# A fused attention and GeGLU kernel: a split opening of the first gate phase, a spare accumulator, and new orders of the attention steps

## The chip, the cores and the metric

The kernel runs on one core of a Trainium2 chip. The metric is the device time of one execution in microseconds (us). Two times are given for it: the median of three plain runs, and the time of one execution that was recorded with a profile. Every row of the profile belongs to that one execution.

## What is computed

Causal attention with 16 always visible "beacon" keys in front, for 8 batches of 8 heads, 576 tokens and head width 64; its output, as 4608 tokens of width 512, goes through a gated feed-forward block with inner width 1536.

```
k_all, v_all = concat([beacon_k, k]), concat([beacon_v, v])
scores = q @ k_all.T / sqrt(64); causal part masked to -1e9
a = softmax(scores)                      # rows sum to 1
x = (a @ v_all) -> tokens x 512
g, val = x @ w_gate, x @ w_val           # 512 -> 1536
out = (gelu(g) * val) @ w_out            # 1536 -> 512
```

## The kernel before, in words

**Tiling.** Tokens are cut into 9 chunks of 512 for the feed-forward part, while attention runs over 8 batches of 576 tokens, so after batch b chunk b is complete. Heads go in four pairs per batch (m = 0 to 3); the two heads of a pair occupy two halves of the array. A chunk's gate phase makes 12 tiles, each of 4 matmuls with `wg_sb` and 4 with `wv_sb` into a two-bank accumulator `gv_ps`; ScalarE takes the Gelu of one bank (`ge_sb`), VectorE multiplies the other by it into `hT_sb` (`gate_val_mms`, `gate_val_end`, lines 365 to 390). The output projection is counted in units of one matmul `o_ps`: 12 units make one output tile of 128 tokens, which VectorE copies to `o_sb` (line 426) and SyncE stores; a chunk has 48 units.

**Attention of a pair** is a list of steps written in strings, one string ("slot") for each pair and one last slot. The letters (function `attention`, line 451):

- `S0` to `S3`: one of four chunks of transposed scores into `s_ps`, then its exp on ScalarE into `expT`. Widths per head are 512, 480, 464 and 208. `s0`, `s2`, `s3` put the scores into the accumulator with the tag `z` instead of the pool `psum_s`.
- For batches from 2 on, GpSimd masks the diagonal blocks behind each exp (line 294). In batches 0 and 1 the masks are steps of their own: `a13` is pair 1, chunk 3 on GpSimd, `d00` one on VectorE by a table.
- `Z`: row sums of the pair before (matmuls with `ones` into `z_ps`, 12, and two with `v_sb`); `I`: their inverse on VectorE (two transposes and a reciprocal); `V`: values into `x_ps`; `M`: the scaling of both into `xT_sb` (line 355). A digit gives the pair.
- `O12`: 12 output units of earlier chunks. `N3`: the next three loads of q and k for the next batch, issued by GpSimd. `h1o`: one matmul `heat` whose result nobody reads.
- `k1z`, `q1x`, `k2o`: TensorE transposes of k or q of one pair for batch 1, into the bank named last; VectorE copies them to `qkT`. From batch 2 on, transposing DMAs on SyncE's queue do this (`xbar_transpose`), issued after the opening of the gate phase.

**Accumulators.** The eight PSUM banks are: pool `psum_s`, two buffers of two banks in turn, for scores and gate tiles; `psum_x`, one buffer `z` of two banks (sums) and one `x` of one bank (values); `psum_o`, one bank `o`. A buffer is free again when its last reader is done.

**Order.** Every engine runs its instructions in the order in which the code issues them. `gate_val_first` (line 397) opens a gate phase: it issues the matmuls of the first `tiles` tiles that need pairs 0 to 2 only, then a filling (`heat` or `o`) of n, then the matmuls that need pair 3. `gate_val` issues whole tiles. GpSimd's queue carries masks and all loads; a load is issued by the instruction at line 115, which waits until the semaphore that it takes from a round of eight is free.

The lines concerned: 365 to 370 (choice of the accumulator of a gate tile), 545 to 552 (gate phase of chunk 0 with two transposes of batch 1, `load_v(1)` and `load_out_w()`), 554 to 571 (the strings of batches 1, 2 and 3 to 7 and the opening of their gate phases), 572 (what is left of the output units).

Of the kernel before, what the change touches and what calls it, by code (L numbers as in the profile page):

```python
# [7 lines left out]
P = 128  # L8
# [5 lines left out]
F_TILES = D_FF // P  # L14
K_CHUNKS = D_MODEL // P
CH = 512
# [29 lines left out]
Z0 = 448  # L46
# [3 lines left out]
FP32 = mybir.dt.float32  # L50
# [8 lines left out]
def kernel(  # L59
# [22 lines left out]
    psum_s = ctx.enter_context(tc.tile_pool(name="psum_s", bufs=2, space=bass.MemoryType.PSUM))  # L82
    psum_x = ctx.enter_context(tc.tile_pool(name="psum_x", bufs=1, space=bass.MemoryType.PSUM))
# [30 lines left out]
    def dma(out_ap, in_ap):  # L114
        keep(nc.gpsimd.dma_start(out=out_ap, in_=in_ap))  # L115
# [8 lines left out]
    def load_runs(b, m):  # L124
        for out_ap, in_ap in runs(b, m):
            dma(out_ap, in_ap)
# [70 lines left out]
    def load_out_w():  # L197
        dma(wo_sb, moe_w_out.rearrange("(ii p) m -> p ii m", p=P))
# [3 lines left out]
    def mm(out_ap, lhsT, rhs, start, stop, **kw):  # L202
        keep(nc.tensor.matmul(out_ap, lhsT, rhs, start=start, stop=stop, **kw))  # L203
# [48 lines left out]
    def trans_in(tag, b, m, w):  # L252
        t_ps = bank(tag, BF16, 1024, "t_ps")
        trans(b, m, w, t_ps, [(S, dve_copy)])
# [3 lines left out]
    def scores(b, m, *chunks, tag="s"):  # L258
        i = b * NPAIR + m
        qkT = qk_ring[b % 2]  # L260
        for c in chunks:
            if c == 0:
                exp_of[i] = epool.tile([P, 2, EXP_W], BF16, name="expT", tag="expT")
            expT = exp_of[i]
            s_ps = (psum_s if tag == "s" else psum_x).tile([P, 2, 512], FP32, name="s_ps", tag=tag)
            for t, s_lo, w, col in CHUNKS[c]:
                for hi in range(2):
                    r = slice(64 * hi, 64 * hi + 64)
                    mm(
                        s_ps[:, hi, col : col + w],  # L270
                        qkT[r, 1, m, t * P : (t + 1) * P],
                        qkT[r, 0, m, NB + s_lo : NB + s_lo + w],
                        True,
                        True,
                    )
            o, w = CHUNK_OFF[c], CHUNK_W[c]
            act(expT[:, :, o : o + w], s_ps[:, :, 0:w], ACT.Exp, scale=QK_SCALE)
            if b > 1:
                mask(b, m, c)
# [42 lines left out]
    def sums(b, m):  # L322
        z_ps = z_of[b * NPAIR + m] = psum_x.tile([P, 1024], FP32, name="z_ps", tag="z")
        attend(b, m, z_ps, Z0, True, 0, SPLIT)
        attend(b, m, z_ps, Z0 + SPLIT, True, SPLIT, S)
        attend(b, m, z_ps, 0, False, 0, SPLIT, start=False)

    def values(b, m):
        x_ps = x_of[b * NPAIR + m] = psum_x.tile([P, S - SPLIT], FP32, name="x_ps", tag="x")
        attend(b, m, x_ps, 0, False, SPLIT, S)  # L330
# [3 lines left out]
    def invert(b, m):  # L334

        i = b * NPAIR + m
        zt = npool.tile([P, S], FP32, name="zt", tag="zt")
        keep(nc.vector.transpose(zt, z_of[i][:, Z0 : Z0 + S]))  # L338
        rz = npool.tile([P, NBLK], FP32, name="rz", tag="rz")
        keep(nc.vector.reciprocal(rz, zt.rearrange("p (n j) -> p n j", j=32)[:, :, 0]))  # L340
        rec = npool.tile([P, S], FP32, name="rec", tag="rec")
        keep(
            nc.vector.transpose(  # L343
                rec.rearrange("p (n j) -> p n j", j=32), rz.unsqueeze(2).to_broadcast([P, NBLK, 32])
            )
        )
        rec_of[i] = rec
# [15 lines left out]
    h_of, gv_of = {}, {}  # L363

    def gate_val_mms(ci, fi, kks):
        if fi == 0 and ci not in h_of:
            h_of[ci] = hpool.tile([P, F_TILES, CH], BF16, name="hT_sb", tag="hT_sb")
        if (ci, fi) not in gv_of:
            gv_of[ci, fi] = psum_s.tile([P, 2, CH], FP32, name="gv_ps", tag="s")
        gv_ps = gv_of[ci, fi]  # L370
        for w in range(2):
            for kk in kks:
                mm(
                    gv_ps[:, w, :],
                    (wg_sb, wv_sb)[w][:, kk, fi * P : (fi + 1) * P],
                    xT_sb[:, kk, ci * CH : (ci + 1) * CH],
                    kk == 0,
                    kk == K_CHUNKS - 1,
                    skip_group_check=True,
                )  # L380

    def gate_val_end(ci, fi):
        gv_ps = gv_of.pop((ci, fi))
        ge_sb = fpool.tile([P, CH], BF16, name="ge_sb", tag="ge_sb")
        act(ge_sb, gv_ps[:, 0, :], ACT.Gelu)
        keep(
            nc.vector.tensor_tensor(  # L387
                out=h_of[ci][:, fi, :], in0=gv_ps[:, 1, :], in1=ge_sb, op=ALU.mult
            )
        )  # L390

    def gate_val(ci, f0, f1):
        for fi in range(f0, f1):
            gate_val_mms(ci, fi, range(K_CHUNKS))
            gate_val_end(ci, fi)

    def gate_val_first(ci, fill, n, tiles=1):

        for fi in range(tiles):
            gate_val_mms(ci, fi, range(K_CHUNKS - 1))  # L400
        fill(n)
        for fi in range(tiles):
            gate_val_mms(ci, fi, [K_CHUNKS - 1])
            gate_val_end(ci, fi)
# [46 lines left out]
    def attention(b, *slots, extra=None):  # L451


        for m, slot in enumerate(slots):
            for step in slot.split():
                kind, n = step[0], step[1:]
                if kind == "S":
                    scores(b, m, *(int(c) for c in n))
                elif kind == "s":
                    scores(b, m, *(int(c) for c in n), tag="z")  # L460
                elif kind == "Z":
                    sums(b, int(n or m - 1))
                    if not n:
                        invert(b, m - 1)
                elif kind == "I":
                    invert(b, int(n))
                elif kind == "V":
                    values(b, int(n or m - 1))
                    if not n:
                        scale(b, m - 1)  # L470
                elif kind == "M":
                    scale(b, int(n))
                elif kind == "O":
                    o(int(n))
                elif kind in "adkq":
                    extra[kind](b, *n)
                else:
                    extra[kind](*n) if kind in "kqrwLhyad" else extra[kind](n)
# [40 lines left out]
    def load_next(n):  # L519
# [4 lines left out]
    extra = {  # L524
        "k": lambda b, m, tag: trans_in(tag, b, int(m), 1),
        "q": lambda b, m, tag: trans_in(tag, b, int(m), 0),
        "a": lambda b, m, c: mask(b, int(m), int(c)),
        "d": lambda b, m, c: mask(b, int(m), int(c), by_table=True),
        "r": lambda m: load_runs(0, int(m)),
        "h": lambda n, tag: heat(int(n), tag),  # L530
        "y": lambda t: load_v_tile(0, int(t)),
        "N": lambda n: load_next(int(n)),
# [3 lines left out]
    for m in range(1, NPAIR):  # L536
# [4 lines left out]
        extra=extra,  # L541
    )
    load_next(99)
    gelu_table()
    gate_val_first(0, heat, 0, 1)
    gate_val(0, 1, 10)
    trans_in("z", 1, 0, 1)
    gate_val(0, 10, 10 + 1)
    trans_in("x", 1, 0, 0)
    gate_val(0, 10 + 1, F_TILES)  # L550
    load_v(1)
    load_out_w()

    for b in range(1, B):
        exp_table()
        if b + 1 < B:
            queue.extend(qk_loads(b + 1))
        if b == 1:
            attention(b, "S0 N3 k1z S1 a01 q1x k3o d00 S2 a02 S3 q2o d03", "N3 S0 S1 k2o Z0 a11 S2 a10 I0 a12 V0 S3 M0", "S0 a13 q3o S1 a21 Z1 S2 h1o a20 I1 S3 a22 V1", "M1 S0 S1 a23 Z2 I2 a31 a30 V2 M2 S2 a32 S3 a33 O12", "Z3 I3 V3 M3 O12 N3", extra=extra)
        elif b == 2:  # L560
            attention(b, "S0 O12 N3 S1 S2 O12 S3 N3", "S0 Z0 S1 S2 I0 O12 S3 N3 V0", "S0 S1 M0 Z1 V1 S2 S3 O6 I1", "S0 M1 S1 Z2 V2 I2 S2 M2 S3", "O2 O4 Z3 V3 I3 N2 M3 O12", extra=extra)
        else:
            attention(b, "O1 s0 S1 O11 s2 S3 N3", "S0 O2 Z0 I0 S1 V0 S2 S3 M0 O10", "S0 S1 Z1 I1 N3 V1 M1 S2 S3 O12", "S0 S1 Z2 V2 S2 I2 S3 M2 N2 O7", "Z3 I3 V3 N3 M3", extra=extra)
        gelu_table()
        if b + 1 < B:
            load_next(99)
            load_v(b + 1)
        gate_val_first(b, o, 0 if b == 1 else 0 if b == 2 else 5)
        if b + 1 < B:
            xbar_transpose(b + 1)  # L570
        gate_val(b, 1, F_TILES)
# [36 lines left out]
```

## Time and profile before

| | us |
|---|---|
| median of three runs | 401.12 |
| lowest and highest of them | 400.2 and 401.52 |
| profiled execution | 399.99 |
| its span, from first to last instruction | 398.3 |

The span is cut below by the start of each phase on TensorE, read from its timeline:

| phase | from | to |
|---|---|---|
| start and attention of batch 0 | 0 | 24.23 |
| gate phase of chunk 0, with two transposes | 24.23 | 47.05 |
| attention of batch 1 | 47.05 | 69.62 |
| gate phase of chunk 1 | 69.62 | 90.44 |
| attention of batch 2 | 90.44 | 115.17 |
| attention of batch 4 | 178.58 | 199.62 |
| after the gate phase of batch 7 | 350.34 | 398.3 |

In the profile PE is TensorE's matmuls, PEld its weight loads, ACT ScalarE, DVE VectorE, POOL GpSimd, SP SyncE. A row of a timeline gives the start, the time to the end of the last of the merged instructions, the engine, the line, the operation, out<-in, the shape of the first, the number of instructions, and in brackets the idle time before it with what ended it. Matmuls are pipelined, so their durations overlap: the distance between starts is what each costs in a run.

These are the costliest groups of ScalarE and VectorE in the attention and gate phases (busy us, mean ns of one, idle before and its releaser):

```profile
L387 DVE TENSOR_TENSOR hT_sb<-gv_ps,ge_sb 128x512 bf16<-128x512 f32 x108 | 74.7, 692 | 116.2 <-ACT ge_sb L206 116.2
L206 ACT ACTIVATE expT<-s_ps 128x1024 bf16<-128x1024 f32 (+3 forms) x128 | 102.8, 865 | 31.9 <-PE s_ps L203 29.0
L338 DVE STREAM_TRANSPOSE zt<-z_ps 128x576 f32<-128x576 f32 x32 | 25.1, 783 | 28.4 <-PE z_ps L203 28.2
```

### The profile page before, as it was taken

The page shows a single profiled execution, that of the slowest core. Times are in us where ns is not written, and L with a number is a line of the kernel's source. Part 1 is how long each engine was busy: PE and PEld are TensorE (multiplying, and loading weights), DVE is VectorE, ACT ScalarE, POOL GpSimd, SP SyncE. Part 2 cuts the span into 40 slices and gives each one's busy share as a digit, 9 for nine tenths or more (in the row PEclk, how much of TensorE's full clock was granted, in tenths as well). Part 3 has the DMA queues.
Part 4 walks back from the last instruction along what each step waited for, and adds up shares of the span by engine and source line. Part 5 has one row for each costly group of instructions (what it writes and reads, how often), then busy time and mean ns, then how long its engine had stood idle before and what let it go on. Part 6 is the DMA issues. An engine that isn't in the chain of part 4 may idle for free.

```text
span 398.3 us, 6685 instructions
## 1 busy us (share of the span) xinstructions
PE 382.4 (96%) x2633; PEld 178.3 (45%) x2674; DVE 197.9 (50%) x339; ACT 188.5 (47%) x255; POOL 164.4 (41%) x299
## 2 busy tenths in 40 slices
PE   7889989999999999999999999999999999999996
PEld 3444444444444444444444444444444444444443
DVE  4863677433663356434653356336643465433332
ACT  4843485236733574338723763357434862322210
POOL 8967268305870078405770379107840330000000
PEclk9999989999999999999999999999999999999999
DMA  9999995945999059994799179915997010000012
GB/s 145 158 206 178 156 96 56 148 86 81 107 113 131 7 81 86 133 112 55 93 128 135 30 72 130 159 21 81 93 161 77 28 53 28 0 26 28 26 59 102
DMA packets 139424, 36.50 MB, mean 92 GB/s; under 512 B 126976, under 2 KB 134912, under 8 KB 139392
## 3 DMA queue, kind: packets, MB, share of 16 engines
q0 software_dynamic: 103696, 18.85, 61.4%
q1 hardware_dynamic: 35552, 17.08, 20.8%
q8 instruction: 21, 0.34, 0.4%
q10 hardware_dynamic: 144, 0.13, 0.1%
q14 instruction: 11, 0.09, 0.1%
HBM read 38.27 MB, written 9.44 MB: 120 GB/s over the span
## 4 chain that ended last, share of the span: by engine, by line
PE 86%; ACT 7%; DVE 3%; issue 1%; DMA 1%; POOL 1%; POOLq 0%
PE gv_ps L203 47%; PE o_ps L203 20%; PE z_ps L203 8%; PE s_ps L203 6%; PE x_ps L203 5%; ACT expT L206 5%; ACT L446 2%; DMA k<-in_k_dram 1%; DVE zt L338 1%; DVE rec L343 1%; ACT ge_sb L206 1%; PE t_ps L224 1%; DVE xT_sb L355 0%; POOL q L115 0%; DVE rz L340 0%
## 5 line engine op out<-in xcount | busy, mean ns | idle before, releaser
L206 ACT ACTIVATE ge_sb<-gv_ps 128x512 bf16<-128x512 f32 x108 | 64.5, 597 | 155.7 <-PE gv_ps L203 153.4
L387 DVE TENSOR_TENSOR hT_sb<-gv_ps,ge_sb 128x512 bf16<-128x512 f32 x108 | 74.7, 692 | 116.2 <-ACT ge_sb L206 116.2
L294 POOL TENSOR_SCALAR_AFFINE_SELECT expT<-expT 128x256 bf16<-128x256 bf16 (+2 forms) x156 | 57.3, 394 | 154.4 <-ACT expT L206 152.5
L206 ACT ACTIVATE expT<-s_ps 128x1024 bf16<-128x1024 f32 (+3 forms) x128 | 102.8, 865 | 31.9 <-PE s_ps L203 29.0
L203 PE MATMUL gv_ps<-xT_sb,wg_sb 128*128 128x512 bf16 x422 | 111.1, 379 | 1.2 <-DVE xT_sb L355 0.8
L203 PE MATMUL gv_ps<-xT_sb,wv_sb 128*128 128x512 bf16 x425 | 111.0, 379 | 0.5
L203 PE MATMUL o_ps<-wo_sb,hT_sb 128*128 128x512 bf16 (+1 forms) x421 | 100.2, 374 | 1.4 <-issue 0.3
L203 PEld LDWEIGHTS <-wv_sb 128*128 128x128 bf16 x432 | 42.3, 98 | 51.9 <-issue 1.0
L203 PEld LDWEIGHTS <-wg_sb 128*128 128x128 bf16 x432 | 41.6, 98 | 50.8 <-issue 1.6
L203 PEld LDWEIGHTS <-hT_sb 128*128 128x128 bf16 x444 | 40.8, 98 | 47.7 <-issue 3.7
L426 DVE COPY o_sb<-o_ps 128x512 f32<-128x512 f32 x35 | 24.2, 690 | 39.6 <-PE o_ps L203 39.6
L203 PE MATMUL s_ps<-qkT 64*128 64x80 bf16 (+5 forms) x384 | 38.7, 283 | 4.7 <-ACT expT L206 3.5
L338 DVE STREAM_TRANSPOSE zt<-z_ps 128x576 f32<-128x576 f32 x32 | 25.1, 783 | 28.4 <-PE z_ps L203 28.2
L115 POOL DMA_DIRECT2D v_sb<-in_v_dram x40 | 33.8, 886 | 0.0
L203 PE MATMUL z_ps<-expT,ones 80*64 80x80 bf16 (+5 forms) x384 | 31.8, 292 | 1.4 <-DVE xT_sb L355 0.2
L203 PEld LDWEIGHTS <-qkT 64*128 64x128 bf16 x384 | 14.4, 94 | 32.0 <-issue 26.8
L203 PE MATMUL x_ps<-expT,v_sb 128*64 128x512 bf16 (+4 forms) x320 | 28.1, 305 | 0.0
L115 POOL DMA_DIRECT2D q_sb<-in_q_dram x30 | 26.0, 865 | 0.5 <-issue 0.2
L115 POOL DMA_DIRECT2D k_sb<-in_k_dram x30 | 25.8, 860 | 0.2 <-issue 0.2
L343 DVE STREAM_TRANSPOSE rec<-rz 128x576 f32<-128x576 f32 x32 | 24.9, 778 | 1.1
L203 PEld LDWEIGHTS <-ones 128*64 128x64 bf16 (+1 forms) x384 | 15.7, 112 | 16.9 <-issue 8.6
L355 DVE TENSOR_TENSOR xT_sb<-x_ps,rec 128x512 bf16<-128x512 f32 x32 | 21.8, 681 | 0.8 <-PE x_ps L203 0.8
(39 smaller groups left out, 122.2 us busy)
## 6 DMA issues: line engine op xcount, KB each, us to landing
out_dram<-o_sb SPq DMA_DIRECT2D x35, 256.0 KB, 2.0
v_sb<-in_v_dram POOLq DMA_DIRECT2D x24, 128.0 KB, 7.2
q_sb<-in_q_dram POOLq DMA_DIRECT2D x24, 128.0 KB, 4.3
k_sb<-in_k_dram POOLq DMA_DIRECT2D x18, 128.0 KB, 4.3
wg_sb<-in_moe_w_gate_dram POOLq DMA_DIRECT2D x3, 512.0 KB, 8.9
wv_sb<-in_moe_w_val_dram POOLq DMA_DIRECT2D x3, 512.0 KB, 10.6
wo_sb<-in_moe_w_out_dram POOLq DMA_DIRECT2D x1, 1536.0 KB, 14.3
q<-in_q_dram POOLq DMA_DIRECT2D x7, 144.0 KB, 5.3
```

Of the source, the lines that this page charges most:

```text
L115: keep(nc.gpsimd.dma_start(out=out_ap, in_=in_ap))
L203: keep(nc.tensor.matmul(out_ap, lhsT, rhs, start=start, stop=stop, **kw))
L206: keep(nc.scalar.activation(out_ap, in_ap, func, **kw))
L224: keep(nc.tensor.transpose(out_ap, in_ap, ident[0:n, 0:n]))
L294: nc.gpsimd.affine_select(out=d, in_=d, pattern=[[0, 2], [1, DIAG[t]]], compare_op=ALU.is_ge, fill=0.0, base=base, channel_multiplier=-1,)
L338: keep(nc.vector.transpose(zt, z_of[i][:, Z0 : Z0 + S]))
L343: nc.vector.transpose(rec.rearrange("p (n j) -> p n j", j=32), rz.unsqueeze(2).to_broadcast([P, NBLK, 32]))
L355: nc.vector.tensor_tensor(out=xT_sb[:, m, b * S + q0 : b * S + q1], in0=acc[:, 0 : q1 - q0], in1=rec[:, q0:q1], op=ALU.mult,)
L387: nc.vector.tensor_tensor(out=h_of[ci][:, fi, :], in0=gv_ps[:, 1, :], in1=ge_sb, op=ALU.mult)
L426: keep(nc.vector.tensor_copy(o_sb, o_ps))
L446: keep(nc.scalar.preload_act_table_set(SET_EXP))
```

## The change

A third tile of chunk 0's gate phase, (0, 2), takes its accumulator from the buffer `z` of `psum_x`. The gate phase of chunk 0 opens with two split tiles for one; the transposes of batch 1's first pair stand two tiles earlier; `wo_sb` is loaded before the values of batch 1. The strings of batches 1, 2 and 3 to 7 are new, one `heat` matmul of batch 1 is dropped, and the gate phase of batch 2 opens with a filling of 5 output units for 0.

```diff
--- before
+++ after
@@ -366,7 +366,10 @@
         if fi == 0 and ci not in h_of:
             h_of[ci] = hpool.tile([P, F_TILES, CH], BF16, name="hT_sb", tag="hT_sb")
         if (ci, fi) not in gv_of:
-            gv_of[ci, fi] = psum_s.tile([P, 2, CH], FP32, name="gv_ps", tag="s")
+            spare = (ci, fi) == (0, 2)
+            gv_of[ci, fi] = (psum_x if spare else psum_s).tile(
+                [P, 2, CH], FP32, name="gv_ps", tag="z" if spare else "s"
+            )
         gv_ps = gv_of[ci, fi]
         for w in range(2):
             for kk in kks:
@@ -542,30 +545,30 @@
     )
     load_next(99)
     gelu_table()
-    gate_val_first(0, heat, 0, 1)
-    gate_val(0, 1, 10)
+    gate_val_first(0, heat, 0, 2)
+    gate_val(0, 2, 8)
     trans_in("z", 1, 0, 1)
-    gate_val(0, 10, 10 + 1)
+    gate_val(0, 8, 8 + 1)
     trans_in("x", 1, 0, 0)
-    gate_val(0, 10 + 1, F_TILES)
+    gate_val(0, 8 + 1, F_TILES)
+    load_out_w()
     load_v(1)
-    load_out_w()
 
     for b in range(1, B):
         exp_table()
         if b + 1 < B:
             queue.extend(qk_loads(b + 1))
         if b == 1:
-            attention(b, "S0 N3 k1z S1 a01 q1x k3o d00 S2 a02 S3 q2o d03", "N3 S0 S1 k2o Z0 a11 S2 a10 I0 a12 V0 S3 M0", "S0 a13 q3o S1 a21 Z1 S2 h1o a20 I1 S3 a22 V1", "M1 S0 S1 a23 Z2 I2 a31 a30 V2 M2 S2 a32 S3 a33 O12", "Z3 I3 V3 M3 O12 N3", extra=extra)
+            attention(b, "k1x S0 N3 S1 a01 k3z d00 q1x S2 a02 s3 q2o d03", "S0 S1 k2o Z0 a11 S2 I0 a12 V0 a10 M0 S3", "a13 S0 q3o S1 a21 Z1 S2 a20 I1 S3 a22 V1", "M1 S0 S1 a23 Z2 I2 V2 a31 M2 a30 S2 a32 S3 d33 O12", "Z3 I3 V3 M3 O12 N3 N3", extra=extra)
         elif b == 2:
-            attention(b, "S0 O12 N3 S1 S2 O12 S3 N3", "S0 Z0 S1 S2 I0 O12 S3 N3 V0", "S0 S1 M0 Z1 V1 S2 S3 O6 I1", "S0 M1 S1 Z2 V2 I2 S2 M2 S3", "O2 O4 Z3 V3 I3 N2 M3 O12", extra=extra)
+            attention(b, "O12 s0 S1 S2 O12 S3 N3", "S0 S1 Z0 I0 V0 M0 S2 S3 O12 N3", "S0 S1 Z1 I1 V1 M1 S2 S3 O12 N3", "S0 S1 Z2 I2 V2 M2 S2 S3 O12 N2", "Z3 I3 V3 M3", extra=extra)
         else:
-            attention(b, "O1 s0 S1 O11 s2 S3 N3", "S0 O2 Z0 I0 S1 V0 S2 S3 M0 O10", "S0 S1 Z1 I1 N3 V1 M1 S2 S3 O12", "S0 S1 Z2 V2 S2 I2 S3 M2 N2 O7", "Z3 I3 V3 N3 M3", extra=extra)
+            attention(b, "O7 s0 S1 S2 O12 S3 N3", "S0 S1 Z0 I0 V0 M0 S2 S3 O12 N3", "S0 S1 Z1 I1 V1 M1 S2 S3 O7 N3", "S0 S1 Z2 I2 V2 M2 S2 S3 O5 N2", "Z3 I3 V3 M3", extra=extra)
         gelu_table()
         if b + 1 < B:
             load_next(99)
             load_v(b + 1)
-        gate_val_first(b, o, 0 if b == 1 else 0 if b == 2 else 5)
+        gate_val_first(b, o, 0 if b == 1 else 5 if b == 2 else 5)
         if b + 1 < B:
             xbar_transpose(b + 1)
         gate_val(b, 1, F_TILES)
```

## The prediction

> **What bounds the kernel now.** I read the page, then the chain of waits, then busy time by stage, then the timeline of each engine around every edited string.
>
> ```profile
> PE 382.4 (96%) x2633; PEld 178.3 (45%) x2674; DVE 197.9 (50%) x339; ACT 188.5 (47%) x255; POOL 164.4 (41%) x299
> PE 86%; ACT 7%; DVE 3%; issue 1%; DMA 1%; POOL 1%; POOLq 0%
> ```
>
> TensorE is the bound: 96% busy and 86% of the chain that ended last. Nothing in the edit removes matmuls worth naming (one `heat` matmul in all), so any gain is gaps in TensorE's stream. The stages show where they are; the columns are window, its length, then busy us (count) of PE, PEld, DVE, ACT, POOL, then clock and DMA. The rows are the attention of batches 1, 2, 4 and 5:
>
> ```profile
> 47.05:69.62 22.57, 20.74 (x244) 10.96 (x245) 16.86 (x33) 15.90 (x19) 14.08 (x28) 0.92 0.91 87
> 90.44:115.17 24.73, 24.02 (x202) 11.17 (x206) 13.96 (x25) 16.22 (x19) 18.75 (x35) 1.00 0.88 92
> 178.58:199.62 21.04, 20.50 (x185) 9.40 (x187) 11.29 (x20) 16.01 (x19) 13.48 (x28) 1.00 0.60 70
> 221.43:242.67 21.24, 20.70 (x186) 9.41 (x187) 11.31 (x20) 16.01 (x19) 13.49 (x28) 1.00 0.59 69
> ```
>
> "Busy" includes pipeline tails, so it hides small gaps. The timeline of TensorE in batch 4 shows them (start, us, what, idle before):
>
> ```profile
> 178.58 0.38 PE L203 MATMUL o_ps<-wo_sb,hT_sb 128*128 128x512 bf16 x1
> 178.89 0.60 PE L203 MATMUL s_ps<-qkT 64*128 64x512 bf16 x8
> 179.42 2.55 PE L203 MATMUL o_ps<-wo_sb,hT_sb 128*128 128x512 bf16 x11
> 181.90 0.46 PE L203 MATMUL s_ps<-qkT 64*128 64x464 bf16 x4
> 182.62 0.39 PE L203 MATMUL s_ps<-qkT 64*128 64x512 bf16 x2 [0.26 <-ACT expT L206]
> 182.95 0.39 PE L203 MATMUL o_ps<-wo_sb,hT_sb 128*128 128x512 bf16 x1
> 183.48 1.14 PE L203 MATMUL z_ps<-expT,ones 128*64 128x64 bf16 x12
> ...
> 189.04 0.91 PE L203 MATMUL z_ps<-expT,ones 128*64 128x64 bf16 x12
> 189.81 0.85 PE L203 MATMUL x_ps<-expT,v_sb 128*64 128x512 bf16 x10
> 190.59 0.61 PE L203 MATMUL s_ps<-qkT 64*128 64x464 bf16 x4
> ```
>
> In a run, full matmuls start every 0.216 us (179.42 to 181.90: eleven, 2.38, plus 0.10). From one output matmul at 178.58 to the scores at 178.89 is 0.31: so **a switch to or from scores costs 0.10 us**. The same 0.10 stands wherever kinds change, except from row sums to values. Clean blocks of a pair: first two score chunks 0.43, sums 0.77, values 0.68, last two chunks 0.28: 2.16, so 8.64 for four pairs; 43 output matmuls 9.28; sum 17.92 of 21.04. The missing 3.1 are 18 switches (1.8) and waits (1.3): 0.43 before 182.62, 0.22 (beyond its switch) before 183.48, 0.2 inside those sums (they last 0.97 to the next row, not 0.77), the rest small.
>
> The opening of chunk 0's gate phase, and the clock in batch 1:
>
> ```profile
> 24.89 0.81 PE L203 MATMUL gv_ps<-xT_sb,wv_sb 128*128 128x512 bf16 x3
> 26.45 0.38 PE L203 MATMUL gv_ps<-xT_sb,wg_sb 128*128 128x512 bf16 x1 [0.76 <-DVE xT_sb L355]
> ```
>
> ```profile
> 52.79:56.20 3.41, 3.41 (x36) 1.87 (x36) 2.19 (x5) 2.35 (x3) 3.09 (x6) 0.50 1.42 93
> ```
>
> Six matmuls (1.29) cannot cover the scaling of pair 3; and 3.41 us of batch 1 run at half clock.
>
> **The skill.** "TensorE: Matmul & The Clock Gate", Part 1, says that an idle activity window of about 3.4 us halves the clock, and that windows are not tied to the kernel's start; the 3.41 us at 0.50 agrees. Part 2 there says that weight loads are pulled ahead of running matmuls when row groups don't conflict or the background buffer takes them; here the 98-ns loads vanish in a run and a like amount (0.10) shows at switches. "DMA: Bandwidth & Descriptors", section "Queues, rings and completion order", says descriptors of a ring are consumed in ring order; the trace agrees: k_sb's first rows, issued 1.0 us after wo_sb, landed just behind it (after 13.5 us, wo_sb after 14.3).
>
> **The change, part by part.**
>
> *Gate opening, chunk 0.* Twelve matmuls now precede the first that needs pair 3: 24.23+2.59=26.82, and DVE delivers at 25.72+0.68=26.40. The gap before 26.45 (0.92: start 25.53 due after six) goes. Next late could be tile 3, which needs tile 0's psum_s slot: tile 0 ends 27.25, Gelu 27.45 to 28.05, multiply to 28.77; tile 2 sits in the z bank (read last by the scaling at 25.6 to 25.8), so tile 3 starts only at 29.41. No wait. Gain **0.92**. Moving the two transposes two tiles earlier is free: their loads landed by 34.3, they start at 38.0.
>
> *wo_sb before v.* The same POOL issues (1.06 for wo_sb, 4.7 for v), so issue time is nil. But POOL reuses eight DMA semaphores in turn: in the built order k_sb's first tile now waits for wo_sb's. Such a wait is visible before:
>
> ```profile
> 30.29 0.63 POOL L115 DMA_DIRECT2D k<-in_k_dram  x1 [1.92 <-DMA wg_sb<-in_moe_w_gate_dram]
> 39.08 1.06 POOL L115 DMA_DIRECT2D wo_sb<-in_moe_w_out_dram  x1
> ```
>
> Issued at 34.4 with 14.3 to land, wo_sb lands near 48.8; then two issues (0.88+0.94) free POOL at 50.6. Queued behind: masks a01 and a02, whose exps end at 50.0 and 50.9, needed by Z0 at 51.8. They fit, by some 0.1. v follows wo_sb in the rings: its loads landed between 38.8 and 43.2 before, 4.4 apart, so the last near 53.3, and values of pair 0 want it at 53.4. Nothing, or up to 1 us late; below nothing is excluded, since v was never late. I take 0.
>
> *Batch 1.* Gate ends at 46.03 (46.95 less 0.92). k1x moves ahead of S0: 46.13 to 46.62, in time that was idle before S1 (0.60 idle at 48.53, waiting for the last Gelu's multiply; that wait stays, to 47.60). Exp starts at 48.14 (Gelu, table 1.28), and exps follow each other by 0.92, 0.85, 0.82, 0.40 (1.89 for the first two together, 1.35 for the last two, less 0.1 overlap): c3 ends 51.27. s3 in the z bank no longer waits for exp c1. S0 of pair 1 waits for q1's copy (DVE: multiply, k1, k3, d00, q1: 50.43): 50.48. k2o to 51.73, Z0 51.83, V0 53.05, S0 of pair 2 54.12, Z1 55.10, V1 56.65, S0 of pair 3 57.45, Z2 58.30, V2 59.13, O12 60.3 to 62.9, Z3 to 64.5, O12 to 67.2. Gate of chunk 1 at 67.2 for 69.62; less the 0.92: **1.5**, at full clock. The eight q/k loads now issued last end at 68.3 (before 68.6), so the transposes, done at about 14 us of SP issue after 71, stay well before batch 2. If a window of 46.8 to 50.2 (by this walk about 0.4 streaming, like the 0.38 that fell before) trips the clock, 1.2 of it comes back.
>
> *Batches 3 to 7.* New order: O7, s0 S1 S2, O12, S3 S0 S1, Z0 V0 and so on: 16 switches for 18 (-0.2). New waits, from the gate's end: O7 to 1.51; its copy on DVE 1.72 to 2.41, so O12 starts at 2.46 for 2.34 (0.12). O12 to 5.05, S3 5.15; its exp 5.42 to 5.96, because S3 stands behind O12; S1 of pair 1 needs that slot: 6.00 for 5.45 (0.55). Z0 then finds all masks. Small ones as before (0.3 to 0.4). Gone are 0.43+0.22+0.21. Sum: 1.6+0.12+0.55+0.4=2.7 for 3.1 to 3.2: about **0.5** each, 2.6 for five. Cover that shrinks: O5 for O7 before Z3 (0.43 less); Z3 at 18.85 needs scaling of pair 2 (18.6) and the last mask. POOL there is dense: from 6.0, a mask, then N3 (2.6) and five masks (1.75) per slot give 19.5 for the last mask, needed at 19.49. Costs 0 to 0.4 each; I take 0. Fill and pair 3's scaling keep their distance (Z3 moves both).
>
> *Batch 2.* Same walk with O12 first: exp starts 1 us later, hidden by output matmuls; waits 0.15 and 0.55; switches 16. Its gaps were 3.2, now 2.7: **0.5**. Five outputs more here (89 done for 84) are five fewer after batch 7 (7 for 12): nil.
>
> Sum 0.9+1.5+0.5+2.6=**5.5**. The profiled execution took 399.99 (span 398.3), so 394.5; the timed runs' median is 401.12, 1.13 above it, so 395.6, which I predict.
>
> **Rivals.**
> *Half clock or late v in batch 1 again.* For: the new slot 0 still idles about 1.5 us in pieces while exps run. Against: fewer, shorter pieces. 1.2 to 2 back: 397.2.
> *The new waits eat the reordering.* Z3 (or Z1, Z2) wait 0.4 each for masks behind N3: batches 2 to 7 give almost nothing; 2.4 to 3 saved: 398.4. For: 0.1 margins. Against: DMA issues were steady at 0.88.
> *Slower: POOL becomes the late engine.* Masks of a slot stand behind N3. If each issue takes longer or waits for its semaphore, the sums of slots 1 to 4 wait. It decides when it costs more than the 5.5 saved plus 1.2: 6.7 over five batches with loads (2 to 6), 1.35 each, 0.45 per late slot. For: 4.4 us of POOL per slot beside 4.1 of TensorE in the short slots. Against: 13.48 of 21.04 busy. Price 2 us each: 405.6.
> *The spare bank gives nothing* (tile 2 waits anyway): 0.9 lost, 396.5; the z bank's reads end a microsecond earlier, so unlikely.
>
> **Numbers.** Forecast 0.52 (own range 393.6 to 396.8), clock or v 0.23, eaten 0.14, slower 0.07, spare bank 0.04. Range 392.8 to 399.2: the lower end is waits of 0.3 per batch that don't appear and a faster batch 1, the upper holds the two mild rivals. A measurement tells 0.3% (1.2 us) from no change. Faster 0.87, same 0.06, slower 0.07.
>
> **What would show it.** Right: the gate's wait near 26.45 gone and its start unmoved; batch 1's attention near 21.2 with clock 1.00; periods of batches 3 to 6 (42.86 from 135.92 to 178.78) near 42.3; a 0.5 us wait before the second scores of slot 1, none before the first. Wrong: sums waiting for POOL, scores of batch 1 behind v or masks after wo_sb, or a half-clock window at other places.

## The result and the profile after

| us | before | after |
|---|---|---|
| median of six runs each, on one chip | 401.15 | 396.45 |
| lowest and highest | 400.2 and 401.52 | 395.41 and 399.06 |
| ratio, with 95% interval | 1 | 0.9898 [0.9866, 0.9931] |
| profiled execution (span) | 399.99 (398.3) | 399.06 (397.3) |

A run over 1.5% above the fastest of the same kernel counts as slow and is left out of the ratios and medians here, which concerns three runs of experiment 3 alone.

The profiled execution of the changed kernel was the longest of its six, so the two profiles differ by 0.93 us only where the medians differ by 4.7. Reading the two spans alone would mislead; the phases show why. The table cuts both executions at the first gate matmul of each chunk, read from TensorE's timeline.

| stretch on TensorE, us | before | after | saved |
|---|---|---|---|
| start to gate phase of chunk 0 | 24.23 | 28.34 | -4.11 |
| gate phase of chunk 0 | 22.72 | 21.80 | 0.92 |
| its end to gate phase of chunk 1 (batch 1) | 22.67 | 20.91 | 1.76 |
| gate 1 to gate 2 | 45.38 | 44.96 | 0.42 |
| gate 2 to gate 3 (after: five output units, 1.08, more) | 41.77 | 42.54 | 0.31 like for like |
| gate 3 to gate 4 | 42.85 | 42.53 | 0.32 |
| gate 4 to gate 5 | 43.05 | 42.54 | 0.51 |
| gate 5 to gate 6 | 42.85 | 42.53 | 0.32 |
| gate 6 to gate 7 | 42.85 | 42.38 | 0.47 |
| gate 7 to the end (after: the five units fewer) | 69.90 | 68.81 | 0.01 like for like |

All edited stretches together saved 5.0 us. The stretch ahead of them, whose code is identical in both kernels, took 4.11 us more in this one execution. These rows of TensorE's timeline show the reason, first of the kernel before and then of the one after:

```profile
15.59 0.88 PE L203 MATMUL x_ps<-expT,v_sb 128*64 128x512 bf16 x10
...
20.23 0.85 PE L203 MATMUL x_ps<-expT,v_sb 128*64 128x512 bf16 x10
```

```profile
13.19 1.60 PE L203 MATMUL z_ps<-expT,ones 128*64 128x64 bf16 x12
...
18.60 1.55 PE L203 MATMUL x_ps<-expT,v_sb 128*64 128x512 bf16 x10
...
21.15 0.85 PE L203 MATMUL x_ps<-expT,v_sb 128*64 128x512 bf16 x10
```

The same ten value matmuls take 0.85 to 0.88 us, and 1.55 in the second kernel up to about 20.9 us: TensorE ran at half its clock there. Note that the clock column does not say so. The busy table of the changed kernel by stage follows (window, length, busy us and count of PE, PEld, DVE, ACT, POOL, then clock and DMA); its rows are the start, the gate phase of chunk 0, and the attention of batch 1:

```profile
5.00:20.90 15.90, 15.27 (x164) 8.16 (x161) 9.04 (x18) 10.20 (x14) 13.11 (x24) 1.00 1.31 133
28.34:50.14 21.80, 21.80 (x123) 9.84 (x121) 10.97 (x19) 6.46 (x11) 12.09 (x18) 1.00 1.39 190
50.14:71.05 20.91, 19.10 (x244) 10.05 (x244) 16.90 (x34) 15.81 (x19) 11.87 (x25) 1.00 0.64 52
```

The first row reads 1.00 although its matmuls last nearly double: the column counts as full what lies before the first clock record. The gate phase is now busy for all of its 21.80 us, and batch 1's attention runs at full clock throughout, where before 3.41 us of it were at 0.50.

The two lines of the page that answer to those of before, busy time and the chain that ended last:

```profile
PE 386.0 (97%) x2673; PEld 179.7 (45%) x2673; DVE 197.7 (50%) x340; ACT 188.4 (47%) x255; POOL 163.1 (41%) x298
...
PE 91%; DVE 4%; ACT 2%; DMA 1%; issue 1%; SPq 0%
```

PE's part of the chain went from 86% to 91% and ACT's from 7% to 2%: exps and the Gelu stand less often in the chain that ended last. They still stop TensorE: its waits that an exp ended sum to 3.7 us in 11 places, for 3.5 us in 12 places before, since batches 3 to 7 each lost one such wait and got another. (PE's 386.0 is more than the 382.4 of before in part because matmuls at half clock count as busy for longer: 15.27 us from 5.00 to 20.90, for 13.32 in the kernel before.)

The opening of chunk 0's gate phase, on TensorE's timeline:

```profile
29.64 0.81 PE L203 MATMUL gv_ps<-xT_sb,wg_sb 128*128 128x512 bf16 x3
30.29 0.81 PE L203 MATMUL gv_ps<-xT_sb,wv_sb 128*128 128x512 bf16 x3
30.94 0.38 PE L203 MATMUL gv_ps<-xT_sb,wg_sb 128*128 128x512 bf16 x1
```

The second tile's six matmuls fill the place of the gap, and the first matmul that needs pair 3 starts at 30.94, right behind (0.65 after 30.29), with no wait in brackets.

Attention of batch 4, the same engine; before it began with one output unit, now with seven:

```profile
180.36 1.68 PE L203 MATMUL o_ps<-wo_sb,hT_sb 128*128 128x512 bf16 x7
181.97 0.79 PE L203 MATMUL s_ps<-qkT 64*128 64x512 bf16 x10
182.81 2.75 PE L203 MATMUL o_ps<-wo_sb,hT_sb 128*128 128x512 bf16 x12
185.50 0.48 PE L203 MATMUL s_ps<-qkT 64*128 64x208 bf16 x4
186.37 0.38 PE L203 MATMUL s_ps<-qkT 64*128 64x64 bf16 x6 [0.39 <-ACT expT L206]
...
188.24 0.46 PE L203 MATMUL s_ps<-qkT 64*128 64x464 bf16 x4
...
193.40 0.61 PE L203 MATMUL s_ps<-qkT 64*128 64x464 bf16 x4
...
198.19 1.25 PE L203 MATMUL o_ps<-wo_sb,hT_sb 128*128 128x512 bf16 x5
199.37 1.06 PE L203 MATMUL z_ps<-expT,ones 128*64 128x64 bf16 x12
200.24 0.19 PE L203 MATMUL z_ps<-expT,v_sb 128*64 128x64 bf16 x1
```

The wait before the third scores is gone. One new wait stands in brackets, before the second scores of pair 1 (186.37), as large as walked. Three small ones have to be computed: 181.97 to 182.81 is 0.84, about 0.1 more than the scores and a switch need; the pair of last chunks takes 0.15 longer in the rows of 0.61 than in that of 0.46; the last sums take 0.87 (199.37 to 200.24) where clean ones take 0.74.

### The profile page after: what moved, and what is told of

It is laid out like the page before. It is cut to its first block, busy times and chain, and to the rows that moved or that the text cites. A ratio compares the mean times of both kernels' runs of the same rounds, so it can differ in the third digit from the quotient of the medians.

```text
span 397.3 us, 6726 instructions
## 1 busy us (share of the span) xinstructions
PE 386.0 (97%) x2673; PEld 179.7 (45%) x2673; DVE 197.7 (50%) x340; ACT 188.4 (47%) x255; POOL 163.1 (41%) x298
## 4 chain that ended last, share of the span: by engine, by line
PE 91%; DVE 4%; ACT 2%; DMA 1%; issue 1%; SPq 0%
PE gv_ps L203 47%; PE o_ps L203 24%; PE z_ps L203 7%; PE s_ps L203 6%; PE x_ps L203 5%; ACT expT L206 2%; PE t_ps L224 1%; DVE o_sb L429 1%; DMA p<-in_k_dram 1%; DVE rec L343 1%; DVE zt L338 1%; DVE xT_sb L355 0%; DVE qkT L247 0%; PE heat L203 0%; DVE rz L340 0%
## 5 line engine op out<-in xcount | busy, mean ns | idle before, releaser
L294 POOL TENSOR_SCALAR_AFFINE_SELECT expT<-expT 128x256 bf16<-128x256 bf16 (+2 forms) x155 | 56.4, 395 | 152.3 <-ACT expT L206 150.3
L203 PE MATMUL gv_ps<-xT_sb,wg_sb 128*128 128x512 bf16 x432 | 112.4, 379 | 0.0
L203 PE MATMUL gv_ps<-xT_sb,wv_sb 128*128 128x512 bf16 x432 | 112.4, 379 | 0.0
L203 PE MATMUL o_ps<-wo_sb,hT_sb 128*128 128x512 bf16 (+1 forms) x444 | 101.8, 374 | 0.3
L203 PEld LDWEIGHTS <-hT_sb 128*128 128x128 bf16 x444 | 41.8, 98 | 48.8 <-issue 3.5
L203 PE MATMUL z_ps<-expT,ones 80*64 80x80 bf16 (+5 forms) x384 | 30.8, 294 | 0.7 <-DVE xT_sb L355 0.6
```

The source lines that it names most:

```text
L294: nc.gpsimd.affine_select(out=d, in_=d, pattern=[[0, 2], [1, DIAG[t]]], compare_op=ALU.is_ge, fill=0.0, base=base, channel_multiplier=-1,)
```

## The experiments

Each kernel is the changed kernel with the edit shown, unless a base is named; experiments 9 to 11 each keep the edits of the one before. The medians, with the ratio to the kernel before, run beside them:

| edit | median us (runs) | ratio [95%] |
|---|---|---|
| 1 opening undone | 397.71 (4) | 0.9887 [0.9799, 0.9974] |
| 2 no spare bank | 396.42 (4) | 0.9893 [0.9811, 0.9974] |
| 3 old strings in batch 1 | 397.86 (17 of 20) | 0.9917 [0.9889, 0.9945] |
| 4 old strings in batches 2 to 7 | 398.81 (20) | 0.9944 [0.992, 0.9969] |
| 5 v before wo_sb | 397.15 (6) | 0.9912 [0.9878, 0.9947] |
| 6 fourth chunk earlier | 394.75 (4) | 0.9842 [0.9816, 0.9869] |
| 7 one warming matmul at the start for seven | 397.46 (7) | 0.9915 [0.9882, 0.9948] |
| 8 edits 6 and 5 | 396.97 (6) | 0.9886 [0.9851, 0.9921] |
| 9 edit 8, first output units in another bank | 394.58 (6) | 0.9844 [0.9816, 0.9872] |
| 10 edit 9, unread matmuls in batch 1 | 394.71 (6) | 0.9839 [0.9808, 0.987] |
| 11 edit 10, nine warming matmuls at the start | 393.97 (6) | 0.9836 [0.9803, 0.9868] |

Single executions of one kernel spread over 1 to 6 us, so edits worth 0.2 to 1 us are judged by the phases of the profiles, where identical code repeats to about 0.03 us at the same clock, and not by these medians.

**1. The opening undone.** One split tile as before, no spare bank.

```diff
-            spare = (ci, fi) == (0, 2)
+            spare = False
...
-    gate_val_first(0, heat, 0, 2)
-    gate_val(0, 2, 8)
+    gate_val_first(0, heat, 0, 1)
+    gate_val(0, 1, 8)
```

> The changed kernel with the gate phase of chunk 0 opened with one split tile again and its third tile in the common accumulators (transposes stay two tiles early). My theory: TensorE waits again 0.92 us (0.76 in the row) for the scaling of pair 3 before the seventh matmul; from the first gate matmul of chunk 0 to the first work of batch 1's attention 22.8 us for 21.9. Rival (the opening is worth nothing, because the wait moves to a later tile): 21.9 us, no wait.

TensorE's timeline of this kernel at the opening:

```profile
28.25 0.81 PE L203 MATMUL gv_ps<-xT_sb,wv_sb 128*128 128x512 bf16 x3
29.81 0.38 PE L203 MATMUL gv_ps<-xT_sb,wg_sb 128*128 128x512 bf16 x1 [0.76 <-DVE xT_sb L355]
```

The wait for the scaling of pair 3 is back, with the 0.76 it had before, and the gate phase takes 22.73 us, 0.93 more. Everything later is as in the changed kernel. The opening is worth 0.92 to 0.93.

**2. Two split tiles without the spare bank.**

```diff
-            spare = (ci, fi) == (0, 2)
+            spare = False
```

> The changed kernel with two split tiles, but the third tile in the common accumulators. My theory: the third tile must wait for tile 0's Gelu and multiply, which end 1.0 to 1.1 us after tile 1's last matmul, so the phase takes 22.9 to 23.0 us for 21.9 and the second split tile brings nothing alone. Rival (the spare bank is decoration): 21.9 us.

```profile
27.64 0.38 PE L203 MATMUL gv_ps<-xT_sb,wv_sb 128*128 128x512 bf16 x1
29.00 1.02 PE L203 MATMUL gv_ps<-xT_sb,wg_sb 128*128 128x512 bf16 x4 [0.98 <-DVE hT_sb L390]
```

Here the third tile waits 0.98 us for VectorE's multiply of the first, whose buffer it takes. The phase lasts 22.95: worse than with one split tile (22.73). The split alone only moves the gap; the spare bank lets it vanish. The rival in which the bank gives nothing falls.

**3. Batch 1 in the old strings**, that is, the changed kernel with the line of batch 1 of before:

```diff
-            attention(b, "k1x S0 N3 S1 a01 k3z d00 q1x S2 a02 s3 q2o d03", "S0 S1 k2o Z0 a11 S2 I0 a12 V0 a10 M0 S3", "a13 S0 q3o S1 a21 Z1 S2 a20 I1 S3 a22 V1", "M1 S0 S1 a23 Z2 I2 V2 a31 M2 a30 S2 a32 S3 d33 O12", "Z3 I3 V3 M3 O12 N3 N3", extra=extra)
+            attention(b, "S0 N3 k1z S1 a01 q1x k3o d00 S2 a02 S3 q2o d03", "N3 S0 S1 k2o Z0 a11 S2 a10 I0 a12 V0 S3 M0", "S0 a13 q3o S1 a21 Z1 S2 h1o a20 I1 S3 a22 V1", "M1 S0 S1 a23 Z2 I2 a31 a30 V2 M2 S2 a32 S3 a33 O12", "Z3 I3 V3 M3 O12 N3", extra=extra)
```

> The changed kernel with batch 1's strings of before. My theory: the attention of batch 1 takes 22.4 to 22.7 us for 20.9 where half of the clock falls into it, 21.2 to 21.5 where it does not; the rest of the kernel as in the changed one. Rival (batch 1's gain was only a half-clock window that happened to be absent): 20.9 us without a half-clock window.

The batch took 23.33 us from the end of the gate phase, 2.42 more than with the new strings, but the comparison is not clean. This row is the busy table for 51.66 to 58.49:

```profile
51.66:58.49 6.83, 6.46 (x65) 3.28 (x64) 4.38 (x11) 4.45 (x7) 5.12 (x10) 0.50 1.40 90
```

Twice 3.41 us ran at half clock; such a stretch of 3.41 us at 0.50 is called a half-clock window below. One difference of the strings still shows by itself, a wait that the kernel before has with the same 0.49 at full clock (at 51.00). On TensorE's timeline of this run:

```profile
51.17 0.37 PE L203 MATMUL s_ps<-qkT 64*128 64x464 bf16 x2 [0.36 <-ACT expT L206]
52.03 0.35 PE L203 MATMUL s_ps<-qkT 64*128 64x208 bf16 x2 [0.49 <-DVE expT L291]
```

With the old strings the fourth chunk waits 0.49 behind the third; in the changed kernel, where it goes to the bank `z`, both stand in one row of four matmuls with no wait between. That wait was removed by the strings; what it would have been worth at the end of the batch at full clock, this run does not tell. The profiles of the kernels before and after tell a part of it. These rows are the first scores of pair 1, before and after, both reached at full clock:

```profile
51.84 0.79 PE L203 MATMUL s_ps<-qkT 64*128 64x512 bf16 x8 [0.20 <-ACT expT L206]
```

```profile
54.36 0.39 PE L203 MATMUL s_ps<-qkT 64*128 64x512 bf16 x2 [0.20 <-DVE qkT L247]
```

From the end of the gate phase it is 4.89 us to the first and 4.22 to the second, so 0.67 is the strings' own up to there. By the first sums 0.54 of it is left (5.59 for 6.13). This speaks against the rival in which all of the gain was a missing half-clock window, but does not exclude it: no run shows the old strings at full clock to the end.

**4. Batches 2 to 7 in the old strings**, with the new ones in batch 1: the two other `attention` lines of before, and the old filling.

```diff
-        gate_val_first(b, o, 0 if b == 1 else 5 if b == 2 else 5)
+        gate_val_first(b, o, 0 if b == 1 else 0 if b == 2 else 5)
```

> The changed kernel with the strings of batches 2 to 7 of before and the opening of batch 2 filled with 0 units. My theory: the distance of two gate phases of batches 4 to 6 is 42.85 us for 42.53, batch 2 loses 0.6, in sum about 2.3 us more than the changed kernel. Rival (the steps' order in batches 2 to 7 doesn't matter, since TensorE's work is the same): 42.5 us and no difference.

From gate 1 to the end this kernel took 328.44 us and the changed one 326.29: 2.15 for the six batches. The distances from gate 3 on are 42.85 and 42.86 again, those of before, for 42.53. So the order of these strings is worth what it saves, and nothing else in the change hides behind it. Batch 1, in its new strings, took 23.14 here, since again

```profile
50.98:57.81 6.83, 6.75 (x67) 3.18 (x65) 5.23 (x11) 4.52 (x7) 4.19 (x9) 0.50 1.44 94
```

two half-clock windows fell into it. This sets the price of two windows at 2.23 us (23.14 for 20.91), and shows that the new strings do not exclude them.

**5. v loaded before wo_sb**, as in the kernel before.

```diff
-    load_out_w()
     load_v(1)
+    load_out_w()
```

> The changed kernel with batch 1's values loaded before the output weights again. My theory: nothing in the attention of batch 1 if the values land before they are read (20.9 us as in the profile of the changed kernel, where the start was late); up to 1 us gained if the start is not late, because then values and masks behind the output weights are just in time. Rival (the place of the load matters to TensorE): batch 1's attention over 0.5 us longer or shorter whatever the start.

Batch 1 took 21.60, 0.69 more, with one half-clock window, 50.60 to 54.01, in it:

```profile
47.19:50.60 3.41, 2.47 (x50) 1.50 (x48) 2.15 (x6) 2.97 (x4) 0.00 (x0) 1.00 1.22 195
50.60:54.01 3.41, 3.41 (x43) 1.95 (x44) 2.28 (x7) 3.41 (x5) 1.09 (x3) 0.50 1.59 154
```

In the 3.41 us ahead of it TensorE was busy for 2.47, and its longest waits there were 0.60 and 0.33. The order of the loads was not separated by this run; the next one did that by accident.

**6. The fourth chunk of pair 0 ahead of the last output units**, to take away the 0.56 us before the second scores of pair 1. Of the lines of batch 2 and of batches 3 to 7 the first string alone is shown:

```diff
-"O12 s0 S1 S2 O12 S3 N3"
+"O12 s0 S1 S2 O7 S3 O5 N3"
...
-"O7 s0 S1 S2 O12 S3 N3"
+"O7 s0 S1 S2 O8 S3 O4 N3"
```

> The changed kernel with the fourth score chunk of pair 0 put after 8 of the 12 output units (after 7 in batch 2). My theory: the wait of 0.56 us before the second scores of pair 1 goes, two switches of 0.1 us come; the distance of two gate phases of batches 4 to 6 is 42.2 us for 42.53, about 2 us over six batches. Rival (the stall only moves, to the sums of pair 0 or the next scores): 42.5 us.

TensorE's timeline of batch 4:

```profile
178.68 1.89 PE L203 MATMUL o_ps<-wo_sb,hT_sb 128*128 128x512 bf16 x8
180.50 0.26 PE L203 MATMUL s_ps<-qkT 64*128 64x208 bf16 x2
180.69 1.04 PE L203 MATMUL o_ps<-wo_sb,hT_sb 128*128 128x512 bf16 x4
181.66 0.60 PE L203 MATMUL s_ps<-qkT 64*128 64x512 bf16 x8
```

The wait is gone (all eight scores in one row), two switches of 0.10 have come, and the distances fell from 42.53 to 42.34: 0.2 of the 0.33 expected, since 0.15 moved to the last chunk of the next slot. The order of the steps is still worth something.

In this execution the start ran at full clock (first gate matmul at 24.11, close to the 24.23 that the prediction used), and so it tests wo_sb before v as it was walked. GpSimd's timeline:

```profile
34.84 1.05 POOL L115 DMA_DIRECT2D wo_sb<-in_moe_w_out_dram  x1
...
49.62 0.83 POOL L115 DMA_DIRECT2D k_sb<-in_k_dram  x1 [8.49 <-DMA wo_sb<-in_moe_w_out_dram]
50.45 0.89 POOL L115 DMA_DIRECT2D q_sb<-in_q_dram  x1
51.34 1.07 POOL L294 TENSOR_SCALAR_AFFINE_SELECT expT<-expT 128x256 bf16<-128x256 bf16 x3
```

and TensorE's, around the first sums of batch 1:

```profile
51.50 1.44 PE L203 MATMUL z_ps<-expT,ones 128*64 128x64 bf16 x12
52.74 0.22 PE L203 MATMUL z_ps<-expT,v_sb 128*64 128x64 bf16 x2
```

GpSimd stands 8.49 us behind a load that takes the semaphore of wo_sb, then issues two loads, and only then masks, from 51.34 on. The sums start at 51.50 and last 1.24 to the next row, 0.52 longer than the 0.72 of the changed kernel; the batch takes 21.42 for 20.91, with no half-clock window. So wo_sb before v cost 0.5 us in this execution, whose start is not slow. With v first the wait is absent: in experiment 11, whose first gate matmul came at 25.32, GpSimd issued the same two loads at 40.17 and 40.99 without one, and batch 1 took 20.91. At a start as early as 24.11 the new strings were not seen with v first. In the profile of the changed kernel the same wait is 6.91 us and costs nothing, because there the attention came 4 us later.

**7. The start with less warming.** `heat(7)`, the unread matmuls ahead of batch 0, becomes `heat(1)`.

```diff
-    heat(7)
+    heat(1)
```

> The changed kernel with one warming matmul at the start for seven. My theory: [...]the half clock lasts well into batch 0 in every execution, the first gate matmul stands near 28.3 us (24.2 with a full clock), and the time is about 399 in every run. Rival (the late start of the profiled execution had another cause, such as a late load): first gate matmul near 24 us and times as the changed kernel's.

The first gate matmul came at 28.74 in the profiled execution; half clock lasted to 22.46. Three of the seven times lie between 399.47 and 399.76, the other four between 396.27 and 397.46: the late start that was expected is seen in the profile, but the times do not show it in every execution, so the expectation was met only in part.

**8. Edits 6 and 5 together**, the strings of experiment 6 and this:

```diff
-    load_out_w()
     load_v(1)
+    load_out_w()
```

> Two edits of the earlier runs together: the fourth score chunk of pair 0 inside the output units (batches 2 to 7), and batch 1's values loaded before the output weights. My theory: where the start runs at full clock, batch 1's attention took 21.4 us with the output weights first, because the masks came 0.5 us late behind them; with the values first it is 20.9 us at full clock whatever the start, and 0.7 to 2.2 more when half-clock windows fall into it; the later gate distances stay 42.3. Rival (the load order is free): 21.4 us.

The distances stay at 42.33 and batch 1 at 20.90, but the start was the slow one again (28.19), so the combination was not seen at a full-clock start, and its median, 396.97, shows nothing of experiment 6's gain.

**9. Output units of slot 0 in the value bank.** A new letter puts them into `x`, so that they need not wait for the copy of the seven before.

```diff
+                elif kind == "X":
+                    o(int(n), "x")
...
...
-"O7 s0 S1 S2 O8 S3 O4 N3"
+"O7 s0 S1 S2 X8 S3 O4 N3"
```

(first string of batches 3 to 7, and `X7` in batch 2)

> As before, and the output tile that follows the first one of a batch takes the idle values bank, so that it needn't wait for the copy of the first. My theory: the 0.12 us wait at its start goes in batches 2 to 7 and nothing comes in its place, gate distances 42.2 us for 42.3. Rival: the values of pair 0 then wait for the copy out of that bank, 42.3 or more.

```profile
178.72 0.79 PE L203 MATMUL s_ps<-qkT 64*128 64x512 bf16 x10
179.45 1.90 PE L203 MATMUL o_ps<-wo_sb,hT_sb 128*128 128x512 bf16 x8
```

From the scores to the output units it is 0.73 for 0.84, and the distances are 42.22 to 42.23, 0.11 less. The 0.12 that the prediction had walked as the wait for a copy is this.

**10. Unread matmuls in the waits of batch 1**, to keep its clock up.

```diff
-"k1x S0 N3 S1 a01 k3z d00 q1x S2 a02 s3 q2o d03", "S0 S1 k2o ...
+"k1x S0 N3 h2o S1 a01 k3z d00 q1x h1o S2 a02 s3 q2o d03", "S0 h1x S1 k2o ...
```

> As before, and four matmuls that nobody reads in gaps of the first two slots of batch 1. My theory: no half-clock window falls into batch 1 any more, in any execution, at no cost, since they end before the waits around them do: batch 1's attention 20.9 to 21.1 us, and the spread of the times is less by what these windows cost (0.7 to 2.2). Rival: each costs its 0.2 us and two switches on the path, 21.7 us or more.

```profile
48.03 0.61 PE L203 MATMUL heat<-warm 128*128 128x512 bf16 x2
```

They cost nothing: the batch takes 20.91 with them, since each stands in a wait that is there anyway, the first two in the 0.60 for the last Gelu's multiply, the others in waits of about 0.3 for exps. No half-clock window fell into batch 1 of this execution, but none fell into it in experiment 9 either, and one fell into the start, at 11.75 to 15.17. One profile can't show that none ever will, and neither the median, 394.71 after 394.58, nor the spread, 1.76 after 1.55, shows a gain.

**11. Two warming matmuls more at the start**, the rest as in experiment 10.

```diff
-    heat(7)
+    heat(9)
```

> As before, and nine warming matmuls at the start for seven. My theory: [...]the clock of the start is full more often; the first gate matmul stands between 24.1 and 28.7 us in the profiles so far, and the median falls by up to 1 us, less the 0.4 by which the first transposes may come late. Rival: the start is as often at half clock, or the delay costs as much: no gain.

The first gate matmul came at 25.32 here, as in the run without them, with one half-clock window at 11.44 to 14.85:

```profile
8.03:11.44 3.41, 1.93 (x40) 1.18 (x37) 2.57 (x6) 2.65 (x5) 3.41 (x6) 1.00 1.44 152
11.44:14.85 3.41, 3.41 (x36) 1.80 (x32) 2.23 (x6) 2.48 (x3) 3.41 (x7) 0.50 2.07 137
```

The median is the lowest of all, 393.97, but 0.7 below the run before it lies inside the spread of either. Whether the warming at the start helps stays open. What is settled is that edits 6 and 9 take 0.3 us off each of batches 3 to 7. The medians of experiments 6 and 9 to 11, 394.0 to 394.8, lie below that of the changed kernel, at a ratio of 0.984 to the kernel before; that of experiment 8 does not.

## Why the prediction was right, and where it was not

The prediction said 395.6; the median is 396.45, inside its narrower range of 393.6 to 396.8, and 4.70 were saved where 5.5 were summed.

**Gate opening: right.** 0.92 predicted; 0.92 between the two profiles, 0.93 when undone alone. The walk of what is late next (tile 3, no wait) held too: the phase is busy for its whole length.

**Batch 1: right in size, partly through the clock.** 1.5 were predicted at full clock, the batch ending 21.2 after the gate phase; measured were 1.76 and 20.91. But the profile of before had one half-clock window in this batch. Experiment 5 had one too and took 0.69 more than the changed kernel; so of the 1.76 an estimated 0.7 is the window and 1.1 the strings. No run shows the old strings at full clock throughout, so this split is not shown; what is shown is 0.67 up to the first scores of pair 1 (experiment 3). The prediction's 1.5 had the same weakness: it set a walk at full clock against a measured batch with a window in it, and so counted the window's absence as a gain of the strings. The times do not separate the two either: at a mean clock of 0.998 or more, the runs with the old strings took 395.35, 396.07 and 397.66, those of the changed kernel 395.41 to 399.06. The prediction's 1.2 for a returning window was too much for one (0.69) and half of what two cost (2.23).

The windows were no accident of one execution, though. A mean granted clock is listed with every run; one window of 3.41 us at 0.50 lowers it by 0.004 over some 396 us. It was 0.998 or more in 7 of 62 runs of the kernel before and in 3 of 20 with the old strings of batch 1 (experiment 3), but in 10 of 20 with the new ones beside it (experiment 4), in 4 of the 6 of the changed kernel, and in 31 of 56 of all the kernels with the new strings and seven warming matmuls. Experiment 8 alone, with 1 of 6, is like the kernels with the old strings. A mean does not tell where in the run a window falls; taken together they agree with the reading that the new strings, which leave shorter waits, make half-clock windows rarer without excluding them.

**wo_sb before v: the margin failed.** "They fit, by some 0.1" was the step: wo_sb landing near 48.8, masks in time for the sums. In experiment 6, at the start that the prediction had assumed, GpSimd came free of the wait only at 49.62 and of the two issues behind it at 51.34, for the 50.6 walked, so the masks came late and the sums lost 0.52. The wait itself had been walked; three sizes were off, all the same way: the issue of wo_sb (34.84 for 34.4), its time to land (14.5 for 14.3), and the start of the sums (51.50 for 51.8). With a margin of 0.1 that was enough. That v might land late was not what cost: the semaphore that one large load holds did. In the profiled execution of the changed kernel the cost was hidden by the late start.

**Batches 3 to 7: the mechanism right, the term too large.** Every new wait stood where it was walked. The 0.55 before the second scores of pair 1 put them 6.00 us behind the gate's end; they came at 186.37, 6.01 after 180.36. The 0.12 before O12 is 0.11 by experiment 9. The old waits for exps and masks are gone. Yet about 0.5 each was forecast and 0.31 to 0.51 came. In batch 4 the attention took 21.04 before and 20.72 after; over the clean 17.92 that is 3.12 and 2.80. So the 2.7 of the prediction was low by 0.1, and "2.7 for 3.1 to 3.2" was then rounded up to 0.5; the gain is a difference of two such sums, and so a tenth in one of them is a fifth of it. (Where 0.51 came, the batch of before had lost 0.2 more than the others.) The small waits that remain, 0.15 twice for the fourth chunk and 0.13 inside the last sums, are the ones that the prediction took as "0.3 to 0.4" or at nothing.

The last of these belongs to GpSimd. Its timeline of the changed kernel, before the last sums:

```profile
195.72 0.90 POOL L115 DMA_DIRECT2D q_sb<-in_q_dram  x1
196.60 0.89 POOL L115 DMA_DIRECT2D k_sb<-in_k_dram  x1
197.46 0.90 POOL L115 DMA_DIRECT2D q_sb<-in_q_dram  x1
198.34 1.76 POOL L294 TENSOR_SCALAR_AFFINE_SELECT expT<-expT 128x224 bf16<-128x224 bf16 x5
```

Three issues of 0.9 and five masks, ending at 200.10, while the sums that read them run from 199.37 to 200.24. The cost is 0.13, of the "0 to 0.4" left open. Batch 7 shows the same strings without loads to issue: its masks end at 327.48, its last sums take 0.74 (326.98 to 327.72), and its distance, gate 6 to gate 7, is 42.38 for 42.53. So it gained 0.47, where batches 3, 4 and 6 gained 0.31 to 0.32. So the rival in which the new waits eat the reordering had its place right and its price too high by three times; the slower rival, which needed 0.45 per slot, had at most this. The rival in which the spare bank gives nothing fell with experiment 2.

**Batch 2** gave 0.42 for 0.5.

**The start was taken as unmoved.** "Its start unmoved" named the gate's start, and by code it is. By clock it was not: 28.34 for 24.23. It added nothing to the forecast of the median, but it made the one profiled execution useless as a total. The median's shortfall against 395.6 is 0.85; of it 0.5 is the sum of the phases (5.0 for 5.5: 0.7 less in batches 3 to 7 and 0.1 less in batch 2, 0.3 more in batch 1), and the rest (0.35) lies within what the clock moves from one execution to the next.

## What to carry to other kernels

Compare two profiles phase by phase, cut at an instruction that both have: a start that identical code passes in 24 or in 28 us will cover any gain of 1 to 4 us. A second split tile removes a wait only if a buffer for the third tile is free as well; look for a pool that is idle in that phase. When a gain is the difference of two sums of small waits, write its error as that of both sums; and before moving a large load forward on a queue with few semaphores, find the instruction that takes that load's semaphore next and what stands behind it.

## What the hardware showed that was not expected

**The clock of the start differs between executions of the same code.** In the profiles of the kernels whose start is the same (all but experiments 7 and 11) the first gate matmul came between 24.11 and 28.34 us. In the latest of them TensorE ran at half clock up to 20.9 us.

**A half-clock window needs no idle window ahead of it.** "TensorE: Matmul & The Clock Gate", Part 1, of the Trainium skill puts the halved clock down to an idle window of about 3.4 us; further on in the same part it also tells of a kernel whose short idle times between groups of matmuls made the clock go up and down. The length agrees: the half-clock windows here are of 3.41 us, one to three in a row (three in experiment 1, 11.07 to 21.31). A whole idle window is not seen ahead of them: in the 3.41 us before the one of experiment 5 TensorE was busy for 2.47 with waits of at most 0.60, and before that of experiment 11 for 1.93. So stretches of short matmuls with waits between them can be followed by one. The busy time alone does not decide, though. Experiment 9 issues the same instructions up to the end of batch 1 as experiment 5, and it had a stretch of the same busy time at nearly the same place (from 0.3 us behind the end of the gate phase, there from 0.2 ahead of it), with full clock behind it:

```profile
47.80:51.21 3.41, 2.47 (x57) 1.62 (x56) 2.69 (x7) 3.38 (x4) 0.00 (x0) 1.00 1.16 170
51.21:54.62 3.41, 2.94 (x57) 1.68 (x55) 2.74 (x6) 3.41 (x6) 1.10 (x4) 1.00 1.58 160
```

What does decide stays open.

**The windows are not a property of the code alone.** They came with old and new strings of batch 1, and in the same code in one execution and not in another (batch 1 of experiment 4 and of the changed kernel, and of experiments 5 and 9).
